# Attention and a feed-forward block on one core: joint scores for rounds 1 and 2, early fills on VectorE, the unit matrix inside the plan, wider margins

## The chip, the cores and the metric

The kernel runs on one core of a Trainium2 chip. The metric is the device time of one execution in microseconds (us). Of a kernel timed several times the median counts. TensorE is called PE, VectorE DVE, ScalarE ACT, GpSimd POOL, and SyncE, which issues all DMAs of this kernel, SP.

## The reference

Eight batches of attention with eight heads, 576 positions and 64 values per head. Blocks of 64 positions are masked causally. The output of attention becomes 4608 tokens of 512 values, which go through a feed-forward block (FFN) with 2048 hidden values and the Mish function. Everything is asked in fp32.

```python
scores = scale * np.matmul(q, k.transpose(0, 1, 3, 2))
mask = block_i >= block_j                     # blocks of 64 positions
scores = np.where(mask, scores, -1000000000.0)
attn = np.exp(scores - np.max(scores, axis=-1, keepdims=True))
attn = attn / (np.sum(attn, axis=-1, keepdims=True) + 1e-09)
x = np.matmul(attn, v)                        # heads joined: (4608, 512)
h = x @ w_in                                  # (512, 2048)
sp = np.where(h > 20.0, h, np.log1p(np.exp(np.minimum(h, 20.0))))
out = (h * np.tanh(sp)) @ w_out               # (2048, 512)
```

## The kernel before

Numbers are split into two halves of 16 bits (hi and lo), and three 16-bit matmuls replace one in fp32. Tokens are worked in 16 tiles: each batch has one tile of 384 and one of 192 tokens. A tile's first FFN product is `m1` (L1539), its Mish on ACT (L1568) frees the accumulation buffer in PSUM (`acc`, three of them) into `Et`, `split` makes hi and lo into `Gt`, and `m2` (L1644) makes the output.

Attention is worked by pairs of heads, four pairs per batch. Batch 0 is done in fp32 straight from the loaded values (`load_own`, `attend`): its queries, keys and values lie in one large buffer, `Et`, which the FFN uses later. For a pair of batch 0, PE makes scores by query (L983), DVE takes their maxima (L1013), PE makes scores by key (L1054) and subtracts the maxima with small matmuls against a scaled unit matrix (`unit_msc`, L1093), ACT takes exponentials (L1111), and PE multiplies with the values (L1126).

The 28 pairs of batches 1 to 7 go through `load_pair` and `attend_pair`. There the scores of a pair are made in three rounds (L1189, and L1201 for hidden blocks). The two heads lie on the two halves of PE's rows, so these matmuls use 64 rows each and two run beside one another. Each round takes one of two score buffers in PSUM (`ss`, the ring `ss_ring`); DVE takes the round's maxima (L1226, L1234), ACT its exponentials (L1260), which free the buffer. The exponentials of round 0 wait for round 0's maxima, those of rounds 1 and 2 for the maxima of round 2. Casts and differences follow (L1292, L1309), then a transposing DMA (L1316, for part of round 1 also L1331) and the product with the values (L1363), and the division (L1426, L1427).

Nothing runs in the order in which the source lists it. Every piece of work is an operation (`add`) with an engine, a duration, what it comes after and which buffers it takes and frees. `Plan.order` simulates all engines, with due times from the table `DUE` as priorities, and repeats that backwards and forwards; the start times found are the order in which each engine gets its instructions. On the chip each engine keeps to that order and waits by semaphores. In the simulation a DMA lands `BEGIN` + its transfer + `DONE` after it is issued, and a freed buffer can be taken again at once. Durations that the plan is given have no effect on the chip but through that order.

Ahead of the plan stand the fills of buffers and the unit matrix: three fills of parts of `Et` on POOL (L399, L401, L402), fills on DVE (L410 to L482), and `make_identity` (its lines are masks.py:197 and 199, on POOL), of which ACT makes two scaled copies, `minus` and `unit_msc` (L522, L523). `Plan` and `order` are the scheduler; its constants are among the lines that the diff shows.

Of the kernel before, what the change touches and what calls it, by code (L numbers as in the profile page):

```python
# [30 lines left out]
    "w": ((-81.5, -95.5, 364.5, 417), (403, 390.5, -32, 490)),  # L31
    "batch": (-57, 311, 226.5, 427.5, 692, 522, 471, 718.5),
    "load": (
        (-55.5, 119, -103.5, -16),
        (-133.5, 18, -64, -70),
        (-2.5, 356.5, 227.5, 243.5),
        (329.5, 137.5, 357, 93),
        (298.5, 511, 289, 368),
        (546, 508.5, 655.5, 1055.5),
        (587.5, 527.5, 707, 681.5),  # L40
        (734.5, 834.5, 641, 915.5),
        (651.5, 689.5, 646, 1051.5),
    ),
    "tile": (
        (-137.5, -64.5, -211, -68, -123, -112.5, -102, -87.5,
         -17, 282.5, -10.5, 13.5, 286, 268, 264.5,
         -49, 270.5, 355.5, 239.5, 449, 275, 238),
        (-66, 355, 330.5, 402, -61, -47.5, 390, 392,
         -65, 307, -51, 375, 484.5, 417, 590,
         319, 572, 508, 521.5, 491.5, 558.5, 375.5),  # L50
        (402, 283.5, 518.5, 288, 402.5, 483.5, 121, 209.5,
         685.5, 408, 474, 644, 414, 648, 598.5,
         415.5, 524, 367, 344, 380, 312.5, 382.5),
        (383.5, 397.5, 315.5, 475, 335, -0.5, 137.5, 363.5,
         74, 422, 236, 605, 90, 296.5, 121,
         345.5, 537, 474, 433.5, 43, 404.5, -215),
        (290, 373, 429.5, 351, 195, 356.5, 300, 277.5,
         564, 401, 297, 394.5, 583.5, 225.5, 571,
         687.5, 385, 273.5, 897, 360, 635.5, 589.5),
        (440.5, 308, 215.5, 619, 692, 607.5, 368, 436.5,  # L60
         504.5, 602, 584, 679, 778, 360, 722.5,
         539.5, 580, 848, 523.5, -35, 642, 451),
        (439, 610.5, 589, 451.5, 585, 685, 396, 620.5,
         748, 589, 750.5, 960.5, 651.5, -69.5, 414,
         513, 676, 747, 602.5, 427.5, 704.5, 633.5),
        (361.5, 316.5, 629, 278.5, 358.5, 389.5, 389.5, 641.5,
         520.5, 585, 473.5, 695, 737.5, -157, 584,
         715, 688.5, 818, 598, 4, 837, -39),
        (502.5, 911, 760.5, 588.5, 539, 446.5, 685.5, 588,
         490, 690.5, 463.5, 649, 601.5, -4, 802,  # L70
         721, 497, 745, 792, 660.5, 703, 788),
        (546.5, 684.5, 652.5, 704.5, 746.5, 395.5, 635.5, 573,
         695.5, 811.5, 726.5, 797.5, 683.5, 6, 587.5,
         581, 838.5, 571.5, 678.5, -178.5, 630, -138),
        (748.5, 621, 686, 459.5, 764, 626.5, 952.5, 859,
         654, 598, 794, 630, 734.5, -1.5, 801,
         759, 766, 664.5, 880, 624, 853, 837),
        (689.5, 906, 777.5, 965, 689, 732.5, 861.5, 967.5,
         790.5, 863, 881.5, 1147.5, 932, 353.5, 770,
         905, 925.5, 920.5, 1061.5, 256.5, 948.5, 313.5),  # L80
        (740.5, 754.5, 866, 913, 1235, 748.5, 861, 1032.5,
         801.5, 704, 748.5, 1037, 992, -76.5, 1118,
         1167, 1113, 1084.5, 742.5, 1081.5, 1080.5, 822),
        (780.5, 1065.5, 795, 817.5, 946, 773, 946, 977,
         962, 1031.5, 918, 1051.5, 1013, 305, 999,
         1150.5, 774, 1023.5, 1019, -182, 954, -99),
        (739.5, 714, 733, 931.5, 881, 839, 1072.5, 887,
         946, 747.5, 1050.5, 1060.5, 949.5, 314, 1080.5,
         1167.5, 941, 1150.5, 843.5, 1122.5, 1088, 1145.5),
        (937.5, 775.5, 1032.5, 1115, 876, 1021.5, 950.5, 950.5,  # L90
         944.5, 938, 895.5, 1100, 1032.5, -48.5, 994.5,
         1112.5, 855, 1173.5, 1197.5, 461.5, 1206, -71.5),
# [30 lines left out]
class Plan:  # L123
# [9 lines left out]
    BEGIN, DONE, FLIGHT = 0.65, 1.1, 8  # L133
# [34 lines left out]
    def go(self, due, back=False):  # L168
# [14 lines left out]
        while events:  # L183
            now = events[0][0]
            while events and events[0][0] <= now:
# [12 lines left out]
                for r in getattr(o, puts):  # L198
                    room[r] += 1
# [142 lines left out]
def attention_moe(  # L342
# [190 lines left out]
    def weight(which, wait, room_free):  # L533
# [13 lines left out]
        for g in range(NG):  # L547
# [86 lines left out]
            if g < PEW[which]:  # L634
# [8 lines left out]
                    [sc] + scaled[-2],  # L643
# [52 lines left out]
    def batch(b):  # L696
# [44 lines left out]
        new["sx"] = add("dve", 0.6, scale_x, [red])  # L741
# [63 lines left out]
    def load_pair(b, p, i, wait_s, wait_u):  # L805
# [57 lines left out]
        def scales():  # L863
# [7 lines left out]
                op1=ALU.mult,  # L871
            )

        sco = add("dve", 0.75, scales, [red])
        s_x = batches[b]["v"][:, 12:13]

        def ends(t):
# [295 lines left out]
    def attend_pair(b, p, st):  # L1173
# [4 lines left out]
        for r, (blocks, far) in enumerate(ROUNDS):  # L1178
            plan.part("tile", 2 * b + r // 2, 2 * p + r % 2)

            def scores(r=r, blocks=blocks, far=far):
# [16 lines left out]
                for col in far:  # L1198
# [610 lines left out]
```

## Time and profile before

| | us |
|---|---|
| median of 3 runs | 1040.0 (1038.88 to 1041.45) |
| the profiled execution, its own time | 1044.65 |
| its span, first to last instruction | 1042.9 |
| PE busy in the span | 1002.0 |
| DVE busy | 667.2 |
| ACT busy | 624.2 |
| POOL busy | 111.1 |

The profile is of one execution. Busy time of PE is the time in which at least one matmul is under way; matmuls overlap, and their ends are modelled. A wait is the idle time of an engine ahead of an instruction, put down to what ended last. The granted clock is PE's share of its full clock, which has two levels here, 0.5 and 1.0.

### The profile page before, as it was taken

To read this page: it belongs to the slowest core of one execution; us is meant where nothing else is said; L and a number is where in the kernel's file an instruction comes from. 1 tells how busy PE (TensorE), PEld (TensorE's weight loads), DVE (VectorE), ACT (ScalarE), POOL (GpSimd) and SP (SyncE) were. 2 spreads that over 40 slices of the span, in tenths; PEclk is the share of its full clock that TensorE was granted. 3 is DMA by queue.
4 is the path that set the end of the run, shared out by engine and by line. 5 is a ranking of instruction groups with operands and counts; after the bars stand their busy time and mean duration, and the time that the engine had idled before them with its cause. 6 is when DMAs were issued, how large, how long until landed. Compare 5 with 4: busy or idle time off the path is not lost.

```text
span 1042.9 us, 25496 instructions
## 1 busy us (share of the span) xinstructions
PE 1002.0 (96%) x10856; PEld 741.7 (71%) x10856; DVE 667.2 (64%) x1279; ACT 624.2 (60%) x1012; POOL 111.1 (11%) x128
## 2 busy tenths in 40 slices
PE   6999999999999999997999999998999999999998
PEld 5767766775867666775767766786668676796687
DVE  3799999766779558976276547785887734331100
ACT  2568797556766556885356567765965755433221
POOL 0102322111111101211021000100311000000000
PEclk7799999999999999999999999999999999999999
DMA  6793538774577618867162635568656520450000
GB/s 208 255 249 99 162 75 164 167 145 108 115 157 147 136 43 183 154 125 163 35 144 75 122 93 109 116 119 162 133 122 143 120 59 17 82 83 21 16 16 24
DMA packets 279538, 121.61 MB, mean 117 GB/s; under 512 B 227200, under 2 KB 265600, under 8 KB 279424
## 3 DMA queue, kind: packets, MB, share of 16 engines
q1 hardware_dynamic: 279424, 119.98, 52.0%
q8 instruction: 85, 1.39, 0.6%
q14 instruction: 29, 0.24, 0.1%
HBM read 55.18 MB, written 9.44 MB: 62 GB/s over the span
## 4 chain that ended last, share of the span: by engine, by line
PE 56%; DMA 7%; DVE 6%; ACT 5%; SPq 4%; issue 2%; POOL 0%; ACTq 0%; DVEq 0%; POOLq 0%
PE acc L1539 26%; PE acc L1644 22%; PE u L1363 5%; PE ss L1189 3%; SPq L1496 3%; DMA PT<-P 3%; ACT pe L1260 2%; DMA kl<-in_k_dram 2%; DMA x_lo<-xt_lo 1%; DVE P L1309 1%; DMA PL<-P 1%; DVE QL L904 1%; DVE VO L904 1%; DMA ql<-in_q_dram 1%; ACT L1260 1%
## 5 line engine op out<-in xcount | busy, mean ns | idle before, releaser
L1644 PE MATMUL acc<-Gt,wo_h 128*128 128x192 f16 (+1 forms) x2048 | 385.5, 287 | 0.9 <-ACT ot L1683 0.9
L1539 PE MATMUL acc<-x_hi,wi_h 128*128 128x192 f16 (+1 forms) x1024 | 294.6, 288 | 12.1 <-ACT Et L1568 10.7
L1539 PE MATMUL acc<-x_lo,wi_h 128*128 128x192 f16 (+1 forms) x1024 | 294.3, 287 | 2.8 <-DMA x_lo<-xt_lo 2.8
L1539 PE MATMUL acc<-x_hi,wi_l 128*128 128x192 f16 (+1 forms) x1024 | 294.3, 287 | 0.0
L1644 PE MATMUL acc<-Gt,wo_l 128*128 128x192 f16 (+1 forms) x1024 | 293.3, 286 | 0.0
L1539 PEld LDWEIGHTS <-wi_h 128*128 128x128 f16 x2048 | 191.8, 98 | 95.6 <-issue 19.0
L1644 PEld LDWEIGHTS <-wo_h 128*128 128x128 f16 x2048 | 187.4, 98 | 54.8 <-issue 5.7
L1568 ACT ACTIVATE Et<-acc,bv 128x384 f32<-128x384 f32 x192 | 108.8, 578 | 130.3 <-PE acc L1539 129.0
L1615 DVE SCALAR_TENSOR_TENSOR Gt<-Et,bv,Gt 128x1536 f16<-128x1536 f32 (+1 forms) x64 | 90.5, 1416 | 113.2 <-ACT Gt L1600 112.8
L1260 ACT ACTIVATE pe<-ss,pv 128x192 f32<-128x192 f32 (+1 forms) x280 | 148.2, 606 | 23.5 <-DVE P L1309 14.8
L1309 DVE TENSOR_TENSOR P<-pe,P 128x1024 f16<-128x1024 f32 x84 | 105.5, 1258 | 38.5 <-ACT P L1297 27.3
L1539 PEld LDWEIGHTS <-wi_l 128*128 128x128 f16 x1024 | 100.6, 98 | 35.4 <-issue 3.2
L1644 PEld LDWEIGHTS <-wo_l 128*128 128x128 f16 x1024 | 100.4, 98 | 33.2
L1226 DVE TENSOR_REDUCE pv<-ss 128x2 f32<-128x384 f32 (+4 forms) x140 | 106.0, 790 | 24.6 <-PE ss L1201 18.5
L1363 PE MATMUL u<-VH,PT 128*128 128x65 f16 x1568 | 83.0, 194 | 7.1 <-DVE tt L1427 3.4
L1363 PEld LDWEIGHTS <-PT 128*128 128x128 f16 x2352 | 79.2, 98 | 12.4 <-DMA PT<-P 4.6
L1292 POOL CAST P<-pe 128x1024 f16<-128x1024 f32 x42 | 55.9, 1330 | 236.8 <-ACT pe L1260 88.9
L1363 PE MATMUL u<-VO,PT 128*128 128x64 f16 x784 | 79.5, 193 | 0.0
L1260 ACT ACT_TABLE_LOAD x46 | 59.0, 1283 | 12.1 <-DVE pv L1234 8.2
L1568 ACT ACT_TABLE_LOAD x49 | 62.9, 1283 | 0.9
L1600 ACT ACTIVATE Gt<-Et,bv 128x1536 f16<-128x1536 f32 (+1 forms) x43 | 54.2, 1262 | 11.3 <-PE acc L1644 10.4
L1683 ACT ACTIVATE ot<-acc,bv 128x192 f32<-128x192 f32 (+1 forms) x42 | 18.8, 480 | 68.8 <-PE acc L1644 59.2
(128 smaller groups left out, 1046.5 us busy)
## 6 DMA issues: line engine op xcount, KB each, us to landing
out_dram<-ot SPq DMA_DIRECT2D x48, 192.0 KB, 2.2
wo_l<-in_w_in_dram SPq DMA_DIRECT2D x8, 1024.0 KB, 6.8
Gt<-in_w_out_dram SPq DMA_DIRECT2D x16, 512.0 KB, 4.5
kl<-in_v_dram SPq DMA_DIRECT2D x28, 288.0 KB, 3.3
ql<-in_q_dram SPq DMA_DIRECT2D x28, 288.0 KB, 3.4
kl<-in_k_dram SPq DMA_DIRECT2D x28, 288.0 KB, 3.8
VL<-in_v_dram SPq DMA_DIRECT2D x28, 192.0 KB, 2.8
VL<-in_v_dram SPq DMA_DIRECT2D x84, 32.0 KB, 2.2
```

The source lines that it names most:

```text
L1189: nc.tensor.matmul(ss[:, 512 * a + col : 512 * a + col + n], lhsT=m[q_][hs, at : at + P], rhs=m[k_][hs, key : key + n], start=first, stop= ...
L1226: nc.vector.reduce_max(out=mx[:, c], in_=ss[:, :, c0:c1], axis=mybir.AxisListType.X)
L1260: nc.scalar.activation(pe[ex[r].slot][:, cols], ss_[S0[r].slot % NSS][:, cols], AF.Exp, scale=esc, bias=mx[:, c, a : a + 1],)
L1292: return lambda: op(out=both()[0], in_=both()[2])
L1309: lambda both=both: nc.vector.tensor_sub(both()[1], both()[2], both()[0]),
L1363: nc.tensor.matmul(out, lhsT=p_, rhs=v_, start=first, stop=True, skip_group_check=True,)
L1496: lambda c=c, j=j, w=w, src=src, dst=dst: nc.sync.dma_start(out=dst[:, :, j : j + w], in_=src[self.half][0:w, c, :], transpose=True,),
L1539: nc.tensor.matmul(pt, lhsT=w[:, d, f * P : (f + 1) * P], rhs=x[:, d, :], start=k == 0 and d == 0 and z == 0, stop=d == NP - 1 and z == 2, ...
L1568: nc.scalar.activation(Et[:, (self.i * NG + g) % NE, j : j + K, 0:n], acc_[c.slot % NACC][:, 0 : K * n].rearrange("p (k n) -> p k n", k=K) ...
L1600: lambda g_hi=g_hi, ev=ev: nc.scalar.activation(g_hi, ev, AF.Copy, scale=self.s_g),
L1615: lambda g_hi=g_hi, g_lo=g_lo, ev=ev: nc.vector.scalar_tensor_tensor(out=g_lo, in0=ev, scalar=self.s_g, in1=g_hi, op0=ALU.mult, op1=ALU.su ...
L1644: nc.tensor.matmul(pt, lhsT=w[:, f, o * P : (o + 1) * P], rhs=g, start=k == 0 and f == 0 and z == 0, stop=f == NF - 1 and z == 2, skip_gro ...
```

## The change

Four things are done. The three early fills of `Et` move from POOL to DVE. The unit matrix becomes an operation of the plan on POOL, with a planned 9.4 us, and its two scaled copies become operations on ACT; what reads them now comes after them in the plan. The scores of a pair's rounds 1 and 2 become one PE operation, which takes both score buffers; round 0 keeps its own. The plan gets a delay `FREE` of 0.4 us before a freed buffer can be taken, and `DONE` of a DMA goes from 1.1 to 1.6 us; some planned durations change by a few hundredths. All due times are new (their table is left out below).

```diff
 DUE = {
...
     LAT, LATPE, OWN = 0.15, 0.2, 0.11
-    BEGIN, DONE, FLIGHT = 0.65, 1.1, 8
+    FREE = 0.4
+    BEGIN, DONE, FLIGHT = 0.65, 1.6, 8
...
+                if done == 3:
+                    for r in getattr(o, puts):
+                        room[r] += 1
+                    continue
...
-                for r in getattr(o, puts):
-                    room[r] += 1
+                if getattr(o, puts):
+                    heapq.heappush(events, (now + (0.0 if back else self.FREE), 3, i))
...
-    nc.gpsimd.memset(Ef[:, :, 2 * S : S + KW], 0.0)
+    nc.vector.memset(Ef[:, :, 2 * S : S + KW], 0.0)
     Ev = Ef[:, :, S + KW :].rearrange("p i (c f) -> p i c f", c=5)
-    nc.gpsimd.memset(Ev[:, :, :, 0 : P + 2 : P + 1], 1.0)
-    nc.gpsimd.memset(Ev[64:P, :, 4, 1 : P + 1], 0.0)
+    nc.vector.memset(Ev[:, :, :, 0 : P + 2 : P + 1], 1.0)
+    nc.vector.memset(Ev[64:P, :, 4, 1 : P + 1], 0.0)
...
-    make_identity(nc, ident)
     minus = P2[1][:, 6 * P : 7 * P]
-    nc.scalar.mul(minus, ident, -1.0)
-    nc.scalar.mul(unit_msc, ident, -MSC)
+    plan.part("w", 0, 0)
+    unit = add("pool", 9.4, lambda: make_identity(nc, ident))
+    units = [
+        add("act", 0.2, lambda o=o, s=s: nc.scalar.mul(o, ident, s), [unit])
+        for o, s in ((minus, -1.0), (unit_msc, -MSC))
+    ]
...
-                    [sc] + scaled[-2],
+                    [sc, units[0]] + scaled[-2],
...
-            Bo = add("pe", products([n for *_, n in pieces]), subtract, [S0] + maxima)
+            Bo = add("pe", products([n for *_, n in pieces]), subtract, [S0, units[1]] + maxima)
...
-            us, work = products([n for _, ps in blocks for _, n, _ in ps] * 3 + [64] * len(far))
-            S0 = st["S"]
-            S0.append(
-                add(
-                    "pe",
-                    (us + 0.27, work),
-                    scores,
-                    st["A"] + [last.get("S")],
-                    take=[ss_ring],
-                )
-            )
-            last["S"] = S0[r]
+        S0 = st["S"]
+        score_ops = []
+        for rs in ((0,), (1, 2)):
+            plan.part("tile", 2 * b + rs[0] // 2, 2 * p + rs[0] % 2)
+            for r in rs:
+                S0.append(add("pe", (0.01, 0.0), lambda: None, [last.get("S")], take=[ss_ring]))
+                last["S"] = S0[r]
+            ns = [n for r in rs for _, ps in ROUNDS[r][0] for _, n, _ in ps] * 3
+            us, work = products(ns + [64] * sum(len(ROUNDS[r][1]) for r in rs))
+            last["S"] = add(
+                "pe", (us + 0.22, work), lambda rs=rs: score(rs), st["A"] + S0[-len(rs) :]
+            )
+            score_ops += len(rs) * [last["S"]]
...
-                    [S0[r]] + maxima[1:],
+                    [score_ops[r]] + maxima[1:],
...
         st["ends"] += ex
+        S0 += score_ops
```

## Rows read from the trace of the kernel before

**Rows 1.** The page's first part: each engine's busy us, share, instructions.

```profile
PE 1002.0 (96%) x10856; PEld 741.7 (71%) x10856; DVE 667.2 (64%) x1279; ACT 624.2 (60%) x1012; POOL 111.1 (11%) x128
```

**Rows 2.** Stretches: length, busy time by engine, granted clock, DMA share, GB/s.

```profile
0.00:20.00 20.00, 11.67 (x66) 8.75 (x67) 3.60 (x22) 4.85 (x9) 2.53 (x17) 0.88 0.50 166
20.00:30.00 10.00, 9.56 (x46) 7.75 (x46) 8.81 (x18) 1.66 (x4) 1.24 (x1) 0.50 1.08 361
100.00:150.00 50.00, 47.00 (x466) 35.12 (x463) 48.91 (x96) 43.73 (x64) 13.94 (x8) 1.00 0.49 122
900.00:1000.00 100.00, 100.00 (x961) 75.43 (x959) 21.47 (x28) 35.31 (x52) 0.00 (x0) 1.00 0.24 47
```

**Rows 3.** PE's waits, to 80 us, then after: sum, times, longest.

```profile
PE acc L983 <- DMA Et<-in_k_dram: 7.1, 2, 4.4
...
PE acc L1539 <- ACT Et L1568: 10.7, 9, 3.0
PE u L1363 <- DVE tt L1427: 3.4, 3, 1.5
PE u L1363 <- DMA PT<-P: 3.1, 3, 1.6
PE acc L1539 <- DMA x_lo<-xt_lo: 2.8, 5, 0.9
PE ss L1189 <- ACT pe L1260: 2.7, 6, 0.7
```

**Rows 4.** SP's DMA queue: the wait of its L788 loads.

```profile
SPq L788 <- POOL Et L402: 9.1, 1, 9.1
```

**Rows 5.** Timeline to 20 us: start, us, instruction, [idle before <- releaser].

```profile
1.66 0.31 DVE L482 MEMSET pe<- 128x128 f32 x2
...
6.60 1.42 DVE L1013 TENSOR_REDUCE PT<-acc 128x1 f32<-128x384 f32 x4 [4.63 <-PE acc L995]
...
9.87 0.28 POOL masks.py:199 TENSOR_SCALAR_AFFINE_SELECT P<-P 128x128 f32<-128x128 f32 x1 [7.37 <-issue]
...
10.21 0.52 POOL L402 MEMSET Et<- 64x512 f32 x1
...
10.76 0.33 SPq L788 DMA_DIRECT2D Et<-in_q_dram  x1
...
14.56 1.69 PE L983 MATMUL acc<-Et 64*128 64x384 f32 x8 [2.68 <-DMA Et<-in_k_dram]
...
16.29 1.46 PE L1093 MATMUL ss<-PT,PT 128*128 128x128 f16 x12
...
19.96 0.69 DVE L572 TENSOR_SCALAR wo_h<-wo_l 128x1024 int32<-128x1024 int32 x1 [9.78 <-DMA wo_l<-in_w_in_dram]
```

**Rows 6.** Line L1539: ns min/median/max, first and last start in us.

```profile
L1539 PE MATMUL acc<-x_hi,wi_h x1024: 243/290/528, 79.8 to 1019.1; 128*128 128x192 f16 x86, 128*128 128x384 f16 x85
```

**Rows 7.** Line L1189 likewise; PE's timeline around one lone round of scores.

```profile
L1189 PE MATMUL ss<-KH,QH x448: 186/206/360, 118.6 to 876.1; 64*128 64x64 f16 x75, 64*128 64x448 f16 x38, 64*128 64x128 f16 x19, 64*128 64x320 f16 x18
...
150.35 0.33 PE L1644 MATMUL acc<-Gt,wo_l 128*128 128x384 f16 x1
150.61 0.39 PE L1189 MATMUL ss<-KH,QH 64*128 64x64 f16 x4
...
151.37 0.50 PE L1644 MATMUL acc<-Gt,wo_h 128*128 128x384 f16 x2
```

**Rows 8.** One stall: timeline at 492 to 494 us, then its stretch.

```profile
492.47 0.68 ACT L852 ACTIVATE QL<-ql 128x576 f16<-128x576 f32 x1 [3.23 <-DMA ql<-in_q_dram]
...
493.77 0.48 PE L1539 MATMUL acc<-x_hi,wi_h 128*128 128x384 f16 x1 [2.96 <-ACT Et L1568]
...
494.00:500.00 6.00, 6.00 (x28) 3.92 (x27) 0.00 (x0) 0.58 (x1) 0.00 (x0) 0.53 0.39 87
```

**Rows 9.** DMA issues: KB each, median us from issue to landing.

```profile
ql<-in_q_dram SPq DMA_DIRECT2D x28, 288.0 KB, 3.4
```

More of the change, by code (lines that the diff above doesn't have):

```diff
@@ L30 @@
 DUE = {
-    "w": ((-81.5, -95.5, 364.5, 417), (403, 390.5, -32, 490)),
-    "batch": (-57, 311, 226.5, 427.5, 692, 522, 471, 718.5),
+    "w": ((-73, 532.5, 437.5, 241.5), (733, 567, 322, 477.5)),
+    "batch": (476, 799, 504, 476, 689.5, 986, 874.5, 854.5),
     "load": (
[L34 to L42, printed above, removed]
+        (347.5, -81, -87, -80),
+        (-36.5, 564.5, -125, 316.5),
+        (642, 315, 14.5, 747.5),
+        (413, 550.5, 338.5, 434.5),
+        (498, 599, 362.5, 748),
+        (397.5, 479.5, 580, 397.5),
+        (694.5, 451, 757, 702.5),
+        (639.5, 529, 880, 693),
+        (640.5, 842, 634.5, 622),
@@ L54 @@
[L54 to L77, printed above, removed]
@@ new lines @@
+        (272, -18.5, 268.5, -45, 366, 274.5, 389, 527.5,
+         283, 4, -2.5, 56.5, 425.5, 32.5, 389.5,
+         534.5, 675, 138, 564.5, 443.5, 315.5, -18.5),
+        (684.5, 413.5, 40, 533.5, 251.5, 419.5, 641.5, 424.5,
+         441, 453, 454, 606.5, 518.5, 261, 363,
+         271.5, 385.5, 297, 498, 582, 531, 478),
+        (-146, 391.5, 439.5, 303, 547.5, 576.5, 347.5, 453.5,
+         425.5, 149, 303, 361, 639.5, -91, 591,
+         356.5, 600.5, 320, 610, -144, 358.5, 120.5),
+        (351, 124, 385.5, 300.5, 239.5, 525.5, 331, 521.5,
+         440, 606.5, 392.5, 461, 736, -127, 513,
+         497.5, 401, 428.5, 477, 853.5, 377, 531.5),
@@ new lines @@
+        (987.5, 752.5, 526, 954.5, 1297.5, 400, 506, 697,
+         554.5, 816, 712.5, 643.5, 783, -104, 538.5,
+         661, 484, 674, 850.5, 725, 583, 638),
+        (549.5, 1092.5, 598.5, 645, 955.5, 1112, 789, 814.5,
+         426, 850, 746, 948, 682, -26, 760,
+         668, 776, 560.5, 676.5, -44.5, 640, 1057),
+        (638, 841, 1076.5, 685.5, 588.5, 461.5, 892.5, 520.5,
+         736, 699.5, 839, 607.5, 585, 325, 605,
+         691, 662, 1059, 931.5, 925, 789, 987.5),
+        (1015, 775.5, 635.5, 955, 626, 938, 861, 841,
+         795.5, 935, 894.5, 867, 916.5, -98.5, 601,
+         1168.5, 784, 840.5, 834, -126, 796.5, 558.5),
@@ L93 @@
+        (710.5, 1149, 1070, 746, 1210, 653.5, 769.5, 986.5,
+         1135, 1280, 1232.5, 884.5, 862.5, 304.5, 1129.5,
+         852, 978, 1167.5, 890, 375, 889.5, -199),
     ),
@@ L739, in scale_x @@
             nc.vector.tensor_scalar_mul(t[:, 3:4], t[:, 14:15], EPS)
-        new["sx"] = add("dve", 0.6, scale_x, [red])
+        new["sx"] = add("dve", 0.75, scale_x, [red])
     def factors(b, w_in_done, w_out_done):
@@ L872, in scales @@
             )
-        sco = add("dve", 0.75, scales, [red])
+        sco = add("dve", 0.6, scales, [red])
         s_x = batches[b]["v"][:, 12:13]
@@ L1030, in attend @@
             us = sum(
-                2 * dve(n, True) if IN_ACC[half] else dve(2 * n, True) for _, n, _ in places
+                2 * dve(n) if IN_ACC[half] else dve(2 * n) for _, n, _ in places
             )
@@ L1114, in attend @@
                 "act",
-                act(W - 64 * half, True) + 0.15 * half,
+                act(W - 64 * half, True) - 0.06,
                 exps,
@@ L1177, in attend_pair, with score @@
         turned, maxima = [], []
-        for r, (blocks, far) in enumerate(ROUNDS):
-            plan.part("tile", 2 * b + r // 2, 2 * p + r % 2)
-            def scores(r=r, blocks=blocks, far=far):
+        def score(rs):
+            for r in rs:
+                blocks, far = ROUNDS[r]
                 ss = ss_[S0[r].slot % NSS]
@@ L1208, in scores @@
                         )
-            us, work = products([n for _, ps in blocks for _, n, _ in ps] * 3 + [64] * len(far))
-            S0 = st["S"]
-            S0.append(
-                add(
-                    "pe",
-                    (us + 0.27, work),
-                    scores,
-                    st["A"] + [last.get("S")],
-                    take=[ss_ring],
-                )
-            )
-            last["S"] = S0[r]
+        S0 = st["S"]
+        score_ops = []
+        for rs in ((0,), (1, 2)):
+            plan.part("tile", 2 * b + rs[0] // 2, 2 * p + rs[0] % 2)
+            for r in rs:
+                S0.append(add("pe", (0.01, 0.0), lambda: None, [last.get("S")], take=[ss_ring]))
[4 more added lines that the diff above has]
+                "pe", (us + 0.22, work), lambda rs=rs: score(rs), st["A"] + S0[-len(rs) :]
+            )
+            score_ops += len(rs) * [last["S"]]
+        for r in range(3):
+            plan.part("tile", 2 * b + r // 2, 2 * p + r % 2)
             def largest(r=r):
@@ L1245, in attend_pair @@
                     "dve",
-                    sum(dve(2 * (c1 - c0), True) for c0, c1, _ in SPANS[r])
-                    + (0.18, 0.18, 0.75)[r],
+                    sum(dve(2 * (c1 - c0)) for c0, c1, _ in SPANS[r])
+                    + (0.12, 0.12, 0.66)[r],
                     largest,
-                    [S0[r]] + maxima[1:],
+                    [score_ops[r]] + maxima[1:],
                     psum=True,
@@ L1271, in attend_pair @@
                     "act",
-                    sum(2 * act(c1 - c0, True) + 0.3 for c0, c1, _ in SPANS[r]),
+                    sum(2 * act(c1 - c0, True) + 0.2 for c0, c1, _ in SPANS[r]),
                     weights,
```

45 lines of the change are left out of this document (21 added, 24 removed).

## The prediction, made before the result was known

> **What bounds the kernel now.** I read the busy shares first, then the table by stage, then who waits for whom, and last the first 35 us row by row. TensorE (PE) is busy 1002.0 of a span of 1042.9 us, the other engines 64% or less [rows 1], so the time is PE's work plus what PE loses. The table by stage [rows 2] shows where it loses. In 0 to 20 us PE is busy 11.67 us at a mean granted clock of 0.88, and from 20 to 30 us that clock is 0.50, the lower of the two levels (1.2 against 2.4 GHz). In 100 to 150 us it is busy 47.00 of 50 while VectorE (DVE) is busy 48.91. From 900 us on it has no gap at all and DVE hardly works. So whatever moves PE's work forward at the start comes off the end, as long as the middle keeps its pace.
>
> The waits [rows 3] give the same sum: in the first 80 us the largest is 7.1 us for the first keys (4.4 of it the very first load, which stays). Behind that the five rows shown add up to 22.7 us: 10.7 for an acc buffer that ScalarE (ACT) frees late, 3.4 for DVE's division, 3.1 + 2.8 for transposing DMAs, 2.7 for a score buffer.
>
> The start has one odd row: SyncE, which issues every DMA, stands 9.1 us behind a POOL memset [rows 4]. The timeline [rows 5] shows why. POOL's triangle selection for the unit matrix (masks.py:199) has 7.37 us of idle time ahead of it and starts at 9.87; the L402 memset is queued behind it and runs 10.21 to 10.73; at 10.76 SyncE issues the second pair's queries, which lie in the buffer Et that this memset writes. Everything behind is late with it: PE stops for the second pair's keys until 14.56, the first subtraction (L1093), in PE's order behind that, starts at 16.29, and DVE sits 9.78 us until its first weight bits at 19.96. The first token tile's FFN matmul starts at 79.8 [rows 6].
>
> **The change part by part.**
>
> *Memsets of Et on VectorE.* The same three fills, about 0.5 us for the longest on POOL [rows 5]. On DVE the nearest row is two 128x128 fills in 0.31, so I take 0.2 to 0.6 each, some 1 us together. DVE's own fills end at 1.97 and its next work starts at 6.60 after 4.63 idle [rows 5], so this 1 us is hidden; uncovered it would cost 1 us. What it gives: SyncE's 9.1 us wait [rows 4] goes, since DVE has nothing long ahead of the fills. The loads behind it, the weights too, go out up to 9.1 us earlier, into a stretch where little is moved.
>
> *Unit matrix in the plan.* The 7.37 us ahead of the selection are not removed: POOL has the same instructions ahead of it, less three fills. So the selection still ends near 10, and with two small scalings on ACT the first subtraction can't start before some 10.4; before, 16.29 [rows 5]. The PE chain of the first pairs comes 16.29 - 10.4 = 5.9 us earlier. Behind the POOL operation nothing is queued that is due so early; ACT's two copies stood in its order before as well, now without being first. The Trainium skill (GPSIMD Engine Reference, 2.1 Instruction dispatch) says that the first call of newly loaded POOL code pays some 6 us with no instruction to see. The trace agrees with its 7.37. By a rule without that cost the front would gain the whole 9.1.
>
> So the front gains 9.1 if the DMAs and DVE alone set it, 5.9 if the unit matrix does, and 0 if another wait steps in. PE worked almost without gaps from 20 to 30 us, at half clock [rows 2], so it is PE's order that set the front, and I take **6.0**. The clock is unknown: fewer gaps may shorten the stretch at the lower level. Half speed in the 10 us of 20 to 30 is worth up to 5; I put nothing in the sum and 5 in the range.
>
> *Scores of rounds 1 and 2 as one operation.* Matmul for matmul PE does the same. What goes is a change from the FFN's 128-row matmuls to the scores' 64-row ones and back. Priced on one lone round [rows 7]: the last FFN matmul starts at 150.35 and streams 384 columns at 2.4 GHz, 0.16 us, to 150.51; the next starts at 151.37, so 0.86 is between. The 12 score matmuls have 6 x 64 + 6 x 448 = 3072 columns, two heads at a time: 1536 / 2400 = 0.64. The change costs 0.22. PE's timeline, from the first score at 118.6 to the last group at 876.1 [rows 7], shows 70 such stretches for 28 pairs: 14 pairs with three, 12 with rounds 0 and 1 already together, 2 with rounds 1 and 2 together. After the change two per pair, 56: 14 x 0.22 = **3.1 us** off PE. Bounds: 0 if the new order pays as much elsewhere, 28 x 0.22 = 6.2 if further neighbours meet. The price is that the operation takes both score buffers: it can't start before round 0's exponentials have freed theirs. Before, only round 2 waited so; those waits are 2.7 us in 6 cases [rows 3]. Round 1's maximum loses its head start beside round 0's exponentials, and its exponentials waited for round 2's maximum anyway. I cost it at 0, because the planner can put FFN matmuls between, with its bound under the rivals.
>
> *Margins and the new order.* FREE, DONE and the changed durations issue nothing on the chip; they move instructions. What they can save is read from one stall [rows 8]: ACT stands 3.23 us for queries whose DMA is late, the Mish that frees an acc buffer is queued behind it, PE stops 2.96 us, and then runs from 494 to 500 at a granted clock of 0.53, some 6 x 0.47 = 2.8 lost. One late load, 5.8 us. The load's median time from issue to landing is 3.4 us [rows 9]; the plan had 0.65 + 1.05 + 1.1 = 2.8 after issue (its own constants, 295 KB at 2.8e5) and gets 3.3, so it fits now. The losses of this kind are 3.1 + 2.8 of DMA waits [rows 3] and this 5.8, 11.7 in all. All due times are new, so which of them stay is not in the trace. I take a third, **4**, for the plan is right about the median load only; bounds -12 (all gone) and +11 (the 22.7 us of [rows 3] grow by half, as an order found anew may have its own late loads).
>
> *Sum.* The profiled execution took 1044.65 us (span 1042.9), 4.65 over the median of the three runs. 1044.65 - 6.0 - 3.1 - 4 = 1031.5, and less 4.65, **1027** for the median.
>
> **The rivals.**
>
> *A, all of it lands.* The front gains 9.1, the switches 3.1, the late loads 11.7: 23.9 us, 1016. For it: PE has no gap after 900 us, so every gain arrives. Against: the unit matrix still comes at 10, and 11.7 needs every load on time.
>
> *B, slower: both score buffers in one hand.* Between round 0's scores and the joint operation stand a maximum on DVE and four exponentials on ACT, and PE takes its order as written: late ACT means that PE stands. The longest single such wait before is 0.7 us [rows 3]; if each of 28 pairs pays that, 28 x 0.7 = 19.6, which less the 9.1 of front and switches gives 1050. It turns slower by 3 us from 12.2 us of new waits, 0.44 per pair. For it: in 100 to 150 us DVE is full [rows 2], and there a maximum is easily late. Against: only 6 of the present waits are of this sort, and the plan now allows 0.4 us for each freed buffer. The Trainium skill (Perfetto Trace Analysis, Matmuls) advises to rotate independent groups through different PSUM banks so that emptying one overlaps the next; the joint operation gives that up for rounds 1 and 2. No row of before shows the cost; by that rule this rival would be the likely one.
>
> *C, the front does not move the end.* The loads go out early, but the first pairs stand for the unit matrix and DVE is full from 50 us on, so the FFN still starts near 79; what is left is the 3.1 of the switches and little from the margins: 1037. For it: DVE's share in [rows 2]. Against: DVE idles till 19.96 for data that now come sooner.
>
> **How the numbers follow.** My forecast (front 6, switches 3, margins 4) gets 0.56, by itself 1018 to 1036; A 0.17, B 0.13, C 0.14. A difference of 0.3%, 3.1 us, is about what a measurement of this kernel tells from none: faster is under 1036.9, slower over 1043.1. Faster: forecast and A, 0.73, with a little of C less a little of the forecast's edge, 0.74. Same: most of C and the mild end of B, 0.14. Slower: the rest of B and of new late loads, 0.12. The range reaches from the neighbourhood of A, 1013, to beyond C, 1042, which leaves out part of A's extreme and most of B.
>
> **What would show it.** Right: no SyncE wait on a POOL fill, the second pair's queries issued before 3 us, the subtraction near 10.4, the first FFN matmul at 71 to 76, DVE's first weight work near 11 to 14; at most 56 score stretches; DMA-caused PE waits after 80 us under 8. Wrong: a first FFN matmul at 78 or later (C); PE waits of the joint operation for ACT of 12 us or more in total (B); a new PE gap of 3 us with the clock falling behind it.

## The result, and the profile of the changed kernel

The changed kernel takes 1030.21 us in the median (4 runs, 1025.3 to 1033.52), the kernel before 1040.72 beside it: ratio 0.989, 95% interval 0.984 to 0.994. The prediction was 1027 in a range of 1013 to 1042. The profiled execution took 1029.63 us, its span is 1027.9.

The table by stage (columns as in [rows 2]):

```profile
0.00:20.00 20.00, 12.79 (x74) 10.38 (x76) 6.36 (x29) 6.34 (x13) 1.67 (x14) 0.91 0.92 307
20.00:30.00 10.00, 10.00 (x92) 7.46 (x92) 8.14 (x15) 3.67 (x8) 0.45 (x1) 0.84 0.99 316
...
100.00:150.00 50.00, 41.57 (x445) 29.12 (x445) 49.35 (x93) 41.86 (x62) 10.19 (x11) 0.96 0.65 144
900.00:1000.00 100.00, 100.00 (x840) 74.94 (x838) 13.54 (x11) 29.84 (x44) 0.00 (x0) 1.00 0.11 25
```

The DMAs of the first 20 us move 307 GB/s where [rows 2] had 166, and PE's clock from 20 to 30 is 0.84 where it was 0.50. In 100 to 150 PE is busy 41.57 us, less than the 47.00 before: DVE is still full there, and something new stands in PE's way. After 900 us PE still has no gap, so what is gained earlier arrives.

The waits: SP's for the fill, then PE's to 80 us, then PE's after (sum, times, longest):

```profile
SPq L797 <- DVE Et L408: 1.0, 1, 1.0
...
PE acc L992 <- DMA Et<-in_k_dram: 4.4, 1, 4.4
PE u L1135 <- ACT pe L1120: 2.5, 1, 2.5
...
PE ss L1198 <- ACT pe L1273: 10.0, 4, 4.2
PE u L1377 <- DMA PT<-P: 4.6, 2, 2.9
PE acc L1553 <- DMA x_lo<-xt_lo: 3.1, 2, 2.0
PE acc L1553 <- ACT Et L1582: 2.8, 5, 1.1
PE acc L1553 <- DMA x_hi<-xt_hi: 0.9, 1, 0.9
```

One more row of before belongs beside [rows 3]:

```profile
PE acc L1539 <- DMA x_hi<-xt_hi: 1.3, 1, 1.3
```

SP's 9.1 us [rows 4] have become 1.0. Against [rows 3], the waits for the Mish (L1553 for ACT) fell from 10.7 to 2.8 us, those for transposing DMAs (PT, x_lo, x_hi) grew from 7.2 to 8.6, and the score operation's wait for ACT grew from 2.7 us in 6 cases to 10.0 in 4.

The start (timeline as in [rows 5]), and the first FFN matmul (as in [rows 6]):

```profile
2.13 0.48 DVE L408 MEMSET Et<- 64x512 f32 x1 [0.16 <-DVE ss L486]
2.65 0.33 SPq L797 DMA_DIRECT2D Et<-in_q_dram  x1
9.24 0.28 POOL masks.py:199 TENSOR_SCALAR_AFFINE_SELECT P<-P 128x128 f32<-128x128 f32 x1 [7.05 <-issue]
...
13.44 0.84 PE L1102 MATMUL ss<-PT,PT 128*128 128x128 f16 x12
14.23 0.74 ACT L733 ACTIVATE P<-Et 128x640 f32<-128x640 f32 x1 [2.08 <-DMA Et<-in_v_dram]
15.95 1.49 ACT L1120 ACTIVATE pe<-ss 128x768 f32<-128x768 f32 x2
16.79 2.83 PE L1135 MATMUL u<-Et,pe 128*128 128x65 f32 x12 [2.51 <-ACT pe L1120]
17.67 0.69 DVE L581 TENSOR_SCALAR wo_h<-wo_l 128x1024 int32<-128x1024 int32 x1 [2.73 <-DMA wo_l<-in_w_in_dram]
```

```profile
L1553 PE MATMUL acc<-x_hi,wi_h x1024: 243/325/368, 72.7 to 1002.1; 128*128 128x192 f16 x86, 128*128 128x384 f16 x85
```

The second pair's queries go out at 2.65 instead of 10.76, and the FFN starts at 72.7 instead of 79.8. But the subtraction comes at 13.44, not 10.4, DVE's first weight bits at 17.67, not at 11 to 14, and there is a new chain: ACT stands 2.08 us for values that it squares (L733, for the batch's scale), its exponentials are queued behind that, and PE waits 2.51 us for them. The order on ACT has a part in it: four squares of values stand ahead of the changed kernel's first exponentials, two ahead of those of the kernel before, and it is the third that waits. The chain was in the trace of before as well, in a row that the prediction did not read. ACT's row there, its first square of values:

```profile
16.25 0.74 ACT L724 ACTIVATE P<-Et 128x640 f32<-128x640 f32 x1 [5.55 <-DMA Et<-in_v_dram]
```

ACT stood 5.55 us; its first exponentials started at 17.84. There the chain ended level with the one that the prediction read: the subtraction, which the exponentials need as well, ended at 17.75 [rows 5].

### The profile page after: what moved, and what is told of

Its sections match the earlier page's. It is cut to its first block, busy times and chain, and to the rows that moved or that the text cites. A ratio compares the mean times of both kernels' runs of the same rounds, so it can differ in the third digit from the quotient of the medians.

```text
span 1027.9 us, 25486 instructions
## 1 busy us (share of the span) xinstructions
PE 991.5 (96%) x10856; PEld 736.8 (72%) x10856; DVE 667.9 (65%) x1286; ACT 632.8 (62%) x1018; POOL 102.1 (10%) x119
## 4 chain that ended last, share of the span: by engine, by line
PE 63%; DVE 22%; issue 4%; DMA 4%; ACT 3%; SPq 2%; POOL 1%; DVEq 0%; ACTq 0%; POOLq 0%
PE acc L1553 28%; PE acc L1658 22%; PE u L1377 5%; DVE pv L1239 4%; DVE P L1322 3%; PE ss L1198 3%; DMA PT<-P 2%; DVE Gt L1629 2%; PE u L1135 1%; SPq L1510 1%; DVE Gt L598 1%; DMA Et<-in_v_dram 1%; DVE QL L913 1%; DVE tt L1441 1%; DVE VO L913 1%
## 5 line engine op out<-in xcount | busy, mean ns | idle before, releaser
L1553 PE MATMUL acc<-x_hi,wi_h 128*128 128x192 f16 (+1 forms) x1024 | 294.6, 288 | 3.7 <-ACT Et L1582 2.8
L1553 PE MATMUL acc<-x_lo,wi_h 128*128 128x192 f16 (+1 forms) x1024 | 294.3, 287 | 3.1 <-DMA x_lo<-xt_lo 3.1
L1553 PE MATMUL acc<-x_hi,wi_l 128*128 128x192 f16 (+1 forms) x1024 | 294.3, 287 | 0.0
L1553 PEld LDWEIGHTS <-wi_h 128*128 128x128 f16 x2048 | 191.1, 98 | 79.9 <-issue 7.5
L1629 DVE SCALAR_TENSOR_TENSOR Gt<-Et,bv,Gt 128x1536 f16<-128x1536 f32 (+1 forms) x64 | 93.0, 1456 | 132.4 <-ACT Gt L1614 131.9
L1553 PEld LDWEIGHTS <-wi_l 128*128 128x128 f16 x1024 | 100.6, 98 | 34.3 <-issue 1.1
L1322 DVE TENSOR_TENSOR P<-pe,P 128x1024 f16<-128x1024 f32 x84 | 102.4, 1222 | 34.8 <-ACT P L1310 30.0
L1614 ACT ACTIVATE Gt<-Et,bv 128x768 f16<-128x768 f32 (+1 forms) x49 | 60.5, 1235 | 10.1 <-PE acc L1658 9.1
L1305 POOL CAST P<-pe 128x1024 f16<-128x1024 f32 x33 | 45.0, 1362 | 207.6 <-ACT pe L1273 79.2
L1697 ACT ACTIVATE ot<-acc,bv 128x192 f32<-128x192 f32 (+1 forms) x49 | 22.4, 487 | 58.9 <-PE acc L1658 48.4
```

The costliest lines, as they stand in the source:

```text
L1305: return lambda: op(out=both()[0], in_=both()[2])
L1322: lambda both=both: nc.vector.tensor_sub(both()[1], both()[2], both()[0]),
L1553: nc.tensor.matmul(pt, lhsT=w[:, d, f * P : (f + 1) * P], rhs=x[:, d, :], start=k == 0 and d == 0 and z == 0, stop=d == NP - 1 and z == 2, ...
L1614: lambda g_hi=g_hi, ev=ev: nc.scalar.activation(g_hi, ev, AF.Copy, scale=self.s_g),
L1629: lambda g_hi=g_hi, g_lo=g_lo, ev=ev: nc.vector.scalar_tensor_tensor(out=g_lo, in0=ev, scalar=self.s_g, in1=g_hi, op0=ALU.mult, op1=ALU.su ...
L1697: evac(lambda o, i, s: nc.scalar.activation(o, i, AF.Copy, scale=s))
```

## The experiments

Two theories on the total. Theory L: the loads at the start give nearly all, the rest nets to little. Theory T: it is the new order (joint scores, margins, due times) that gives. Ratios are to the kernel before in runs on the same chip.

**The fills alone.** The kernel before with nothing but the three fills on VectorE; every engine's later order is as it was.

```diff
-    nc.gpsimd.memset(Ef[:, :, 2 * S : S + KW], 0.0)
+    nc.vector.memset(Ef[:, :, 2 * S : S + KW], 0.0)
...
-    nc.gpsimd.memset(Ev[64:P, :, 4, 1 : P + 1], 0.0)
+    nc.vector.memset(Ev[64:P, :, 4, 1 : P + 1], 0.0)
```

> The kernel before with its three fills of Et on VectorE and nothing else; each engine's order stays what it was. Theory L (the front gains because the loads go out 8 to 9 us earlier): the second pair's queries are issued before 3 us, the first FFN matmul comes at 71 to 75 us instead of 79.8, and the time falls by 5 to 8 us to 1032 to 1035. Rival O (the new order, not the fills, made the front shorter; in the changed kernel PE's idle time in the first 80 us is 10.1 against 11.2 us, almost the same): the first FFN matmul stays at 78 or later and the time within 2 us of 1040. Rival C (what counts is the granted clock, 24 us at the lower level before against 13.6 after): the gain is as large as half of the time by which the stretch at the lower level shrinks, and nothing if it does not shrink.

Measured: 1028.16 us (1026.79 to 1029.5), ratio 0.988 (0.985 to 0.991): as fast as the whole change, and more than expected; the first FFN matmul, expected at 71 to 75, comes at 66.9. Its timeline and first FFN matmul:

```profile
10.18 0.31 ACT L522 ACTIVATE P<-P 128x128 f16<-128x128 f32 x1 [8.18 <-POOL P masks.py:199]
10.59 0.72 ACT L724 ACTIVATE P<-Et 128x640 f32<-128x640 f32 x1
12.74 0.69 DVE L572 TENSOR_SCALAR wo_h<-wo_l 128x1024 int32<-128x1024 int32 x1 [2.56 <-DMA wo_l<-in_w_in_dram]
12.92 0.84 PE L1093 MATMUL ss<-PT,PT 128*128 128x128 f16 x12
13.47 1.51 ACT L1111 ACTIVATE pe<-ss 128x768 f32<-128x768 f32 x2 [1.21 <-PE ss L1093]
```

```profile
L1539 PE MATMUL acc<-x_hi,wi_h x1024: 243/323/524, 66.9 to 1002.5; 128*128 128x192 f16 x86, 128*128 128x384 f16 x85
```

The unit matrix comes as late as ever (its copies start at 10.18), yet the FFN starts at 66.9, and ACT no longer stands for values ahead of the exponentials. So theory L holds for the total, and the rest of the change nets to nothing on top. That left two questions: why the changed kernel's FFN starts 5.8 us later than this one's, and what the new order does behind it.

**One fill late again.** The changed kernel with the fill L408 back on POOL, behind the selection.

```diff
-    nc.vector.memset(Ev[64:P, :, 4, 1 : P + 1], 0.0)
...
+    def unit_and_fill():
+        make_identity(nc, ident)
+        nc.gpsimd.memset(Ev[64:P, :, 4, 1 : P + 1], 0.0)
+    unit = add("pool", 9.4, unit_and_fill)
```

> The changed kernel with the L408 fill of Et issued on POOL right behind the unit matrix, so that the loads into Et stand some 9 us again; the plan's order is untouched. Theory L: first FFN matmul at 78 to 80 us instead of 72.7, time up by 6 to 7 us to 1036 to 1037. Rival O: first FFN matmul at 74 at most, time within 2 us of 1030. Rival C: the loss is half of what the stretch at the lower clock grows by.

Measured: 1035.11 us (8 runs, 1032.09 to 1037.68), ratio 0.995 (0.994 to 0.997), 4.9 us over the changed kernel by the medians, some 6 by the ratios (expected 6 to 7). Its waits of SP and PE, and ACT's start:

```profile
SPq L801 <- POOL Et L530: 9.6, 1, 9.6
...
PE u L1139 <- ACT pe L1124: 6.5, 1, 6.5
```

```profile
18.89 0.74 ACT L737 ACTIVATE P<-Et 128x640 f32<-128x640 f32 x1 [7.77 <-DMA Et<-in_v_dram]
```

A fill of half a microsecond puts SP's wait back (9.6), through it the values (ACT stands 7.77), through that the exponentials (24.09) and PE's products; the FFN starts at 79.5. The whole chain is in one trace. The second pair's keys are late with it: PE's waits for keys are 7.6 us, 4.4 in the changed kernel. Rival C falls: PE's time at the lower clock before 80 us is 17.1 us here and 13.7 in the changed kernel, half of that growth is 1.7, and the FFN's start moved by 6.8.

**The joint operation taken apart.** In the changed kernel round 2's scores are issued behind the next FFN or value product, with the plan left as it is.

```diff
...
+            last["S"].parts = [lambda r=r: score((r,)) for r in rs]
...
+            if len(getattr(o, "parts", ())) == 2:
+                o.parts[0]()
+                open_, seen = o, 0
+                continue
             o.emit()
+            if open_ and o.eng == "pe" and o.emit.__name__ in ("prods", "values"):
+                open_.parts[1]()
+                open_ = None
...
```

> The changed kernel, in whose order the joint operation is issued in two parts: round 1's scores at its place, round 2's behind the next FFN or values operation of PE (or before round 2's maximum, if that comes first). Nothing else moves. Theory S (each stretch of 64-row matmuls among 128-row ones costs 0.22 us on PE): 84 stretches instead of 56, PE pays 28 x 0.22 = 6.2 us, and the time goes up by 4 to 7 us, as PE has no gap in the last 120 us. Rival H (PE's idle time of 36 us elsewhere hides it): within 2 us of 1030.

Measured: 1032.54 us (1031.39 to 1035.19), ratio 0.993 (0.990 to 0.995), 2.3 over the changed kernel by the medians, some 4 by the ratios. That is little more than such medians differ by: those of the kernel before, beside the different experiments, lie between 1039.27 and 1041.86. In the trace PE's timeline has 84 score stretches instead of 56, and from the first FFN matmul to the end 961.2 us instead of 955.2. These 6.0 us are not all switches: while PE has work in that stretch, the split kernel spends 13.7 us at the lower clock, the changed one 6.8. The price itself is in the rows of a pair without a wait and at the full clock, split and then joint: the last FFN matmul ahead of each score stretch, and the first behind it.

```profile
175.95 0.33 PE L1659 MATMUL acc<-Gt,wo_l 128*128 128x384 f16 x1
...
177.09 0.50 PE L1659 MATMUL acc<-Gt,wo_h 128*128 128x384 f16 x2
177.42 0.33 PE L1659 MATMUL acc<-Gt,wo_l 128*128 128x384 f16 x1
...
178.44 0.50 PE L1659 MATMUL acc<-Gt,wo_h 128*128 128x384 f16 x2
```

```profile
178.57 0.33 PE L1658 MATMUL acc<-Gt,wo_l 128*128 128x384 f16 x1
...
180.37 0.50 PE L1658 MATMUL acc<-Gt,wo_h 128*128 128x384 f16 x2
```

Less 0.16 for each last FFN matmul, as in the prediction, the split rounds take 1.14 + 1.02 - 0.32 = 1.84 us and the joint ones 1.80 - 0.16 = 1.64: 0.20 for one more switch, where 0.22 was expected, and 28 x 0.20 = 5.6 us for all. The score operation's waits for ACT went back to 4.5 us. So the switches' price is borne out by the trace; the median gives less of it.

**PE kept busy in the old gap.** The kernel before with 70 idle matmuls in the stretch in which PE waited for the second pair.

```diff
...
+            for _ in range(70):
+                nc.tensor.matmul(
+                    u_[0][:, 0:64], lhsT=far_q, rhs=far_k, start=True, stop=True
+                )
...
```

> The kernel before, with 70 idle matmuls of 128 rows and 64 columns behind the first pair's scores, into a PSUM tile that nobody has used yet; their results are overwritten. They fill the gap from 12 to 14.6 us in which PE waits for the second pair's keys. Fills, loads and order stay as before. Rival C: the clock does not fall at 15.0 us or comes back sooner than 38.9, and the first FFN matmul comes 5 to 10 us earlier, at 70 to 75, though no load is earlier. Theory L: the loads set the front; first FFN matmul at 79 to 81, time within 2 us of 1040.

Measured: 1040.44 us (10 runs), ratio 1.001 (0.999 to 1.002): nothing. The profiles say why this can't settle the clock. The stages of this kernel:

```profile
0.00:20.00 20.00, 12.18 (x130) 9.40 (x130) 3.49 (x21) 4.10 (x9) 2.54 (x17) 1.00 0.47 154
20.00:30.00 10.00, 9.62 (x58) 7.86 (x60) 8.61 (x17) 2.74 (x7) 1.02 (x1) 0.66 1.08 358
```

and those of a second execution of the kernel before, profiled to compare:

> The kernel before once more, for a second trace: the first one is of an execution of 1044.65 us, some 4.5 over the median. Theory: the front is alike (first FFN matmul at 79 to 80 us, lower clock for 17 to 24 us of the first 40), and the difference to the first trace lies behind it, in PE's stalls of 2 to 3 us with the clock falling after them (before: at 493 and 718 us). Rival: the front itself varies by some us from run to run, so that the 7.1 us between the two kernels' first FFN matmuls are partly chance.

```profile
0.00:20.00 20.00, 12.61 (x74) 9.32 (x74) 3.81 (x21) 4.85 (x9) 2.53 (x17) 1.00 0.50 168
20.00:30.00 10.00, 6.42 (x46) 5.04 (x46) 8.70 (x17) 1.99 (x5) 0.92 (x1) 0.66 1.07 360
```

That second execution (1038.68 us) has the same clock, 1.00 and 0.66, without any added matmul, where [rows 2] had 0.88 and 0.50, and both start the FFN at 76.1, where 79 to 81 were expected. So the rival holds: of the 7.1 us between the two kernels' first FFN matmuls 3.7 can be chance. In the unchanged kernel the clock of the front is a matter of the single execution; the trace on which the prediction rests was one of the slower ones.

**The joint operation without a new plan.** The order of the fills-alone kernel, with round 1's scores held back until round 2's.

```diff
...
+            if r == 1 and held.get(id(pair), ()) is not None:
+                held.setdefault(id(pair), []).append(o)
+                continue
+            if what == "s" and r == 2:
+                first, *rest = held.get(id(pair), [])
+                first.emit()
+                o.emit()
+                for x in rest:
+                    x.emit()
...
```

> e1_fills_alone (the old order, fills of Et on VectorE), in whose order round 1's scores and their maximum wait until round 2's scores are due, so that both rounds are one stretch on PE; nothing else moves, no due time and no margin changes. Theory S: 56 to 58 stretches instead of 71, 14 x 0.22 = 3.1 us less than e1's 1028.2, so 1025. Rival B (both score buffers in one hand; round 1's maximum now comes later on a full VectorE): PE's waits of the scores for ScalarE, 3.7 us in e1, grow by 3 us or more, and the time is that of e1 or above, 1028 to 1034.

Measured: 1042.95 us (10 runs), ratio 1.002 (0.999 to 1.005): 14.8 us over the fills alone, and over the 1028 to 1034 of rival B. PE's timeline has 56 score stretches, as meant. PE's waits after 75 us, here and then in the fills-alone kernel:

```profile
PE acc L1541 <- ACT Et L1570: 14.7, 15, 2.4
PE u L1365 <- DVE tt L1429: 5.6, 7, 2.5
PE ss L1189 <- ACT pe L1262: 5.1, 8, 2.0
```

```profile
PE acc L1539 <- ACT Et L1568: 9.9, 8, 2.4
PE u L1363 <- DVE tt L1427: 2.2, 3, 1.4
PE ss L1189 <- ACT pe L1260: 3.7, 4, 2.3
```

All three grow, by 4.8, 3.4 and 1.4 us. So the fewer switches (3.1) are no gain by themselves in an order that was made for three rounds. Rival B has the direction right, but not the mechanism: the wait that it names, the scores for ACT, was to grow by 3 us or more and grew by 1.4; the rest is lost in waits behind it. That 14.8 + 3.1 = 17.9 lies near the 19.6 of the prediction's rival B is chance, for that sum was made of this one wait. Nor is the buffer shown to be the cause: the run also moves round 1's maximum on VectorE, and no run separates the two.

**Old due times, and old margins.** Two kernels take one ingredient of the new order back: the old table of due times with the new margins, and the new table with the old margins (FREE 0, DONE 1.1).

```diff
-    FREE = 0.4
+    FREE = 0.0
-    BEGIN, DONE, FLIGHT = 0.65, 1.6, 8
+    BEGIN, DONE, FLIGHT = 0.65, 1.1, 8
```

> The changed kernel with the old table of due times: joint scores, margins, unit matrix in the plan and fills on VectorE all stay. Theory T (the due times were found for one set of operations and margins, and the margins alone move the order away from it): slower than the changed kernel by 10 us or more, 1040 to 1060, with PE waits after 80 us well over 22 us. Rival M (the margins are what makes an order good on the chip, whatever the due times): within 5 us of 1030.

> The changed kernel with FREE at 0 and DONE at 1.1 again; due times, joint scores, unit matrix and fills stay as changed. Theory T: as the due times were found with the margins, the order without them is worse by 10 us or more, 1040 to 1060. Rival M: worse by up to 5 us through DMA waits of PE, which rise over the 8.6 us of the changed kernel.

Measured: 1052.14 us (5 runs, ratio 1.009, 1.007 to 1.012) and 1063.97 us (2 runs, ratio 1.020, 1.015 to 1.025). Largest waits of PE, first with the old due times, then with the old margins:

```profile
PE ss L1063 <- DVE PT L1029: 10.4, 2, 9.8
```

```profile
PE u L1377 <- DVE tt L1441: 15.9, 2, 14.9
PE u L1377 <- DMA PT<-P: 14.8, 7, 4.2
```

In each a few operations came into an order in which PE waits long for them (9.8, 14.9 us in one piece). Theory T has the times right, or nearly (1063.97 is over its range), but for the old due times not the place: PE's waits after 80 us are 25.3 us, hardly more than the changed kernel's 22.4, and it is the first FFN matmul that comes late, at 88.1 instead of 72.7. With the old margins PE's waits for DMAs rose from 8.6 to 21.2 us, as rival M said, but at a far higher price. So neither the new table nor the new margins are good with the other's old value; these runs don't measure what margins are worth by themselves.

**Where the front of the changed kernel loses.** In its order SP issues the queries and keys of the third and fourth pair ahead of the values and of the first weights. Three kernels reorder SP's first 19 loads and nothing else: values and weights both forward, values alone, weights alone.

```diff
     with tc.manual_schedule():
+        free = [o for o in ops if o.eng == "sp" and not o.after][:19]
+        turn = (0, 1, 2, 3, 6, 7, 8, 11, 12, 13, 14, 4, 5, 9, 10, 15, 16, 17, 18)
+        for k in turn:
+            free[k].emit()
         for o in ops:
-            o.emit()
+            if o not in free:
+                o.emit()
```

This is the tuple of the values alone (0 to 3 are the queries and keys of the first two pairs, 4, 5, 9 and 10 those of the next two, 6 to 8 and 11 to 14 values, 15 and 16 the weights). Load 8 is a part of the second batch's values, which goes through the buffer kl; the expectation calls it late keys.

> The changed kernel with the first loads in another order on SyncE and nothing else moved: after the first two pairs' queries and keys come the values of pairs 0, 1 and 2 and the first two loads of w_in, and only then the queries and keys of pairs 2 and 3. In the changed kernel ScalarE waits 2.1 us for the values of a later pair ahead of the first exponentials, TensorE then stands 2.5 us and its clock falls, and VectorE gets its first weights at 17.7 us against 12.7 in e1_fills_alone. Theory L (the front is set by when the data come that stand first in the order of ScalarE and VectorE): first weights on VectorE at 12 to 14 us, first exponentials before 14.5, first FFN matmul at 67 to 70 us instead of 72.7, time 3 to 5 us lower at 1025 to 1027, faster than both kernels. Rival Q (the queries and keys of pairs 2 and 3 are needed as early): TensorE waits for them instead, first FFN matmul at 72 or later and time within 2 us of 1030.

> The changed kernel with its first 19 loads reordered on SyncE: the six value loads of the first batch and the late keys of the first set go out ahead of the queries and keys of the pairs behind the second; the first weights stay behind all of these, as in the changed kernel. It holds half of what the run with all loads turned did. Theory V (what the turned loads gave came from ScalarE, which no longer stood for a value load with the first exponentials queued behind it): exponentials at about 14.5 instead of 15.95, no 2.5 us gap of PE, first FFN matmul at 67 to 69, median 1023 to 1027. Theory W (it came from VectorE, which got its first weights earlier): its first weight bits stay at 17 or later, first FFN matmul at 71 to 74, median 1028 to 1032.

> The other half: only the first two weight loads go out right behind the loads of the second pair; the values stay behind the queries and keys of the later pairs and come 1.1 us later than in the changed kernel. Theory W: first weight bits on VectorE at 12 to 14, first FFN matmul at 66 to 69, median 1023 to 1027. Theory V: ScalarE stands for the value load some 1 us longer, exponentials at about 17, PE's gap ahead of the first products 3 to 4 us, first FFN matmul at 72 to 75, median 1029 to 1034.

Measured: both 1024.5 us (5 runs), ratio 0.985 (0.983 to 0.987); values alone 1025.04 (4 runs), ratio 0.985 (0.981 to 0.989); weights alone 1035.55 (10 runs), ratio 0.994 (0.992 to 0.997). The first two are faster than the kernel before, and by the medians some 5 us faster than the changed one, though there the intervals of the ratios overlap. Values alone and weights alone were timed beside the same runs of the kernel before and are clearly apart. DVE's first weights and ACT's exponentials, values alone and then weights alone, with PE's wait of the latter:

```profile
17.75 0.69 DVE L581 TENSOR_SCALAR wo_h<-wo_l 128x1024 int32<-128x1024 int32 x1 [3.64 <-DMA wo_l<-in_w_in_dram]
13.16 1.51 ACT L1120 ACTIVATE pe<-ss 128x768 f32<-128x768 f32 x2
```

```profile
14.66 0.68 DVE L581 TENSOR_SCALAR wo_h<-wo_l 128x1024 int32<-128x1024 int32 x1
21.67 1.49 ACT L1120 ACTIVATE pe<-ss 128x768 f32<-128x768 f32 x2
```

```profile
PE u L1135 <- ACT pe L1120: 8.4, 1, 8.4
```

With values alone the weights come as late as in the changed kernel (17.75) and the FFN starts at 67.1; with weights alone they come 3 us earlier and the FFN starts at 77.1. Theory V holds, theory W falls: the values decide, through ACT's exponentials (13.16 against 21.67). The clock adds to it: for the same 460 matmuls ahead of the first FFN matmul PE is busy 62.6 us in the changed kernel and 58.6 with the values forward, 4.0 of the 5.6 us between the two starts. Before 80 us the changed kernel spends 13.7 us at the lower clock, which begins at 16.3 inside PE's 2.51 us wait for ACT; the other spends 6.8. The price of the weights ahead of them was mis-sized in the expectation (1 us more of standing; it was 5.7, from 15.95 to 21.67).

All fronts in one table, from each kernel's timeline and span; the tail is the span less the first FFN matmul:

| kernel | ACT's exponentials | DVE's weights | granted clock to 80 us | first FFN | tail |
|---|---|---|---|---|---|
| before, two executions | 17.8, 17.3 | 20.0, 20.8 | 0.85, 0.96 | 79.8, 76.1 | 963.1, 960.7 |
| fills alone | 13.5 | 12.7 | 1.00 | 66.9 | 959.5 |
| changed | 16.0 | 17.7 | 0.91 | 72.7 | 955.2 |
| one fill late | 24.1 | 25.7 | 0.89 | 79.5 | 953.7 |
| both loads forward | 14.5 | 15.3 | 0.96 | 66.4 | 956.3 |
| values forward | 13.2 | 17.8 | 0.96 | 67.1 | 953.4 |
| weights forward | 21.7 | 14.7 | 0.89 | 77.1 | 954.5 |

In the new order the first FFN matmul comes late where ACT's exponentials do, though not one for one, and not where the weights do. In the old order exponentials, weights and clock change together, and the table doesn't separate them.

## Why the prediction was right, and where it was not

The total was close (1027 against 1030.2) and its main step holds: SP's 9.1 us [rows 4] were the cost, and the second pair's queries went out before 3 us. But terms were mis-sized and made good for each other, so that the total came out this close is luck in good part.

- **The front, 6.0.** In the trace it gave 79.8 - 72.7 = 7.1 against the profiled execution and 3.4 against the second one of that kernel. The step that failed is the one that named the unit matrix as the new limit. Its copies start at 10.18 in the fills-alone kernel and PE does not wait for them: it is busy with the second pair's scores until the subtraction, 12.92 there, 13.44 in the changed kernel. So the 5.9 was no bound. The fills alone are worth 1040.1 - 1028.2 = 11.9 us, twice the term and over the 9.1 that I held for the most. The chain that I missed runs from SP through the values to ACT's squares and the exponentials behind them. In the kernel before it ended level with the subtraction, in the changed kernel it sets the front; ACT's 5.55 us row was in the trace. I asked what PE and DVE waited for, not what stood ahead on ACT. The Trainium skill's cost for the first call of POOL code (GPSIMD Engine Reference, 2.1 Instruction dispatch) fits what these traces show, 7.00 to 8.20 us of idle time ahead of the selection; that the idle time is this cost no run shows. Without it the front was to gain 9.1, and more than that came with the idle time still there.
- **What the new order takes back.** I had DVE's weights at 11 to 14; they came at 17.67, for SP's new order puts two more pairs' loads ahead. That I did not go through the loads one by one was a second miss, though not the weights but the values cost time: 72.7 - 66.9 = 5.8 us of the FFN's start. So the first FFN matmul fell into my 71 to 76 for a reason that I did not give. The prediction's rival C is excluded: with the fills alone the end moves as the front does.
- **Clock in the front, 0 in the sum.** PE's timeline has 13.7 us at the lower level before 80 us (two stretches), 23.9 in the trace before, 6.8 in the second execution, none with the fills alone. The idle matmuls don't separate it, but the runs do for the greater part. Seven runs of the kernel before had a mean granted clock of 0.996 to 1.000, as the four of the fills alone beside them had; they took 1035.78 to 1042.22 us (median 1040.63) against 1026.79 to 1029.5. A clock of 0.996 leaves at most 0.004 x 1040, some 4 us, to it. So most of the 11.9 us is earlier work, and how much of the rest is clock stays open.
- **Switches, 3.1.** There are exactly 56 stretches, and the price of one is borne out by the split operation (0.20 in its rows): 14 x 0.20 = 2.8.
- **The joint operation, 0.** It was not nothing: 10.0 us of waits where there were 2.7. One of them was on my list of signs against me, a gap over 3 us with the clock falling behind it (to the lower level at 135.7 us). PE and ACT around it:

```profile
131.49 0.19 PE L1210 MATMUL ss<-far_k,far_q 64*128 64x64 bf16 x2
132.57 1.28 ACT L1273 ACT_TABLE_LOAD   x1
133.86 1.93 ACT L1273 ACTIVATE pe<-ss,pv 128x192 f32<-128x192 f32 x4
135.84 0.61 PE L1198 MATMUL ss<-KH,QH 64*128 64x64 f16 x4 [4.16 <-ACT pe L1273]
```

The first and the last row are of one joint operation. Round 1's half is done at 131.7; round 2's half needs the buffer that round 0's exponentials free, and ACT still has casts, then a table load of 1.28 us and those exponentials. So the step "it can't start before" was the plan's view: on the chip PE starts the operation and then stands inside it. The total stays under the 12 us from which I had B decide, and no more than 4 of the 28 pairs show such a wait. The Trainium skill's advice to rotate matmul groups through PSUM banks (Perfetto Trace Analysis, Matmuls) agrees in direction with the wait for ACT that grew from 2.7 to 10.0 us; but rival B, which it would have made the likely one, did not come true.
- **Margins, 4.** Wrong in place, and not measured by itself. PE's DMA waits after 80 us did not fall under 8: 4.6 + 3.1 + 0.9 = 8.6, before 3.1 + 2.8 + 1.3 = 7.2. What fell is the waiting for the Mish, 10.7 to 2.8. All of PE's waits after 80 us are 22.4 us against 25.3. Whether margins or due times did it, the runs don't separate.
- **Switches, joint operation and margins together** were to give 3.1 + 4 = 7.1. The tails of the three kernels of the old order average 961.1, of the five of the new 954.6: 6.5. Compared on medians, the values-forward kernel against the fills alone, it is (0.988 - 0.985) x 1040, some 3 us, with intervals that overlap. By the tails the sign is right; the size lies between.
- **The profiled execution against the median.** I took 4.65 off for it. Against the second trace its span is 6.1 us longer, 3.7 of them in the front (79.8 against 76.1) and 2.4 in the tail; taking the difference off the total was right, but a front read from that one trace was too long.

So the whole, by medians and single traces, is: fills some 12 us gained, 6 of them lost again to the order of the loads, 3 to 6 gained in the middle. Turning the loads keeps all: 1024.5.

## What to carry to other kernels

At a start, follow the queue that issues the loads: a small fill behind a slow first instruction of another engine can hold every load behind it, and the cost shows up on engines that never touch the filled buffer. Check for each load in a new order what stands in line behind its first reader, for a side task such as a scale's squares can hold the main chain. Try a change's cheapest part alone before crediting the rest, and do not judge a merged operation or a margin under an order that was made without it.

## What the hardware did that I had not expected

Two executions of the same kernel, 0.6% apart, differed by 17 us in how long PE ran at the lower clock in the front (23.9 and 6.8 us), and by 3.7 us in the FFN's start; a single trace is a poor measure of a front. And POOL's selection has 7.00 to 8.20 us of idle time ahead of it in every trace, also where the fills of `Et` are no longer on POOL (7.05 in the changed kernel), so it does not come from these fills.
